# Turning the local q and k of two batches by DMA instead of on TensorE

## The chip, the cores and the metric

The kernel runs on one core of one Trainium2 chip. The metric is the device time of one execution in microseconds (us); lower is better. The time before is 301.74 us, the median of three runs that lie between 301.6 and 302.94 us. The profile is of one more execution.

## The reference

The work is a causal sparse attention followed by a two-layer network. There are 8 batches, 8 heads, 576 positions and 64 numbers per head. Heads 0 to 3 are local (a position sees the 32 positions that end with itself), heads 4 to 7 are strided (it sees the positions before it at multiples of 32).

```python
scores = scale * np.matmul(q, k.transpose(0, 1, 3, 2))
mask_local = (rel >= 0) & (rel < stride)                      # stride = 32, heads 0 to 3
mask_strided = (rel >= 0) & (pos[None, :] % stride == pos[:, None] % stride)   # heads 4 to 7
scores = np.where(masks[None, :, :, :], scores, -1000000000.0)
attn = np.exp(scores - max); attn = attn / (sum + 1e-09)
attn_out = np.matmul(attn, v)
x = attn_out.transpose(0, 2, 1, 3).reshape(4608, 512)
h = x @ w_in                                                  # 512 -> 2048
g = np.maximum(h, 0.0) + alpha * np.minimum(h, 0.0)
out = g @ w_out                                               # 2048 -> 512
```

## The kernel before

Batches, chunks and pairs are counted from 0 here, as the code does. (The change's own short name counts the batch whose load moves as the fourth; it is batch 3 here.)

**The two halves.** The 4608 tokens are cut into nine chunks of 512. Chunk n goes through the first layer in 16 `lin1_piece` calls (four matmuls of 512 columns each, L583; ScalarE makes `neg` at L591, VectorE makes `gT` at L594) and then through the second layer. Chunk 1 does that in 16 calls of `lin2_piece` (L622, four matmuls each); chunks 2 to 8 use `lin2_fast` (L708), which streams fewer columns but also needs the sums `gsum` that VectorE and GpSimd make (L652).

The attention of batch n+1 is done in small pieces between these calls: `attn_step` takes the next piece from a list, and the loop at the end of the kernel spreads the pieces evenly over a chunk. So the order on every engine is written out by hand, instruction by instruction, and each engine runs its own list in that order. An instruction that waits holds up all that stands behind it on its engine.

**Pairs.** Heads are worked on in pairs. Pair g belongs to batch g // 4; of a batch's four pairs, the first two (`hp` 0, 1) are local, the last two (`hp` 2, 3) strided. A pair's pieces are: scores (`score_both`, L353: matmuls of kT and qT, then ScalarE's exponentials at L376 and L382, then GpSimd's mask multiplies at L378 and L385), two or three "PV" pieces (`pv_piece`, L406, with VectorE's L413 and L415 behind), and the turn of the result into `xT`, by DMA transposes (`x_dma`: L446 straight into `xT` for local pairs, L443 into `xs` for pair `hp` 2, which ScalarE then orders into `xT` at L452) or, for `hp` 3, by TensorE and ScalarE (`x_piece`, L429 and L207).

**Where q and k come from.** Scores need q and k with the 64 head numbers on the partitions, so both must be turned. A local pair reads `qTs[0]` and `kTs[0]`; the first local pair of a batch uses half e = 0 of each, the second e = 1. Strided pairs read `qTs[1]` and `kTs[1]`. There are three ways in the kernel:

- Local q and k of batches 0 to 4: a load in fp32 by the SyncE (SP) or GpSimd queue (`load_qk`), a cast to 16 bits (`cast_l`, on GpSimd for batches 3 and 4), nine TensorE transposes for q and nine for k (`transpose_piece`, L269) into two PSUM tiles of the pool `ps` each, and two ScalarE copies each (L207) into `qTs[0]` or `kTs[0]`, which also put the columns in order.
- Local q and k of batches 5 to 7: a casting load on the GpSimd queue (`load_rows`, L116) and four DMA transposes on the SP queue (`turn_rows`, L128) that write `qTs[0]` and `kTs[0]` directly.
- Strided q and k of batches 3 to 7: a casting load of both on the GpSimd queue into `qsd` and `ksd` (`load_d`, L134, one buffer each), and two DMA transposes on the SP queue (`transpose_d`, L175).

**The places in the list.** For each g the list holds the scores of pair g, then the PV pieces of pair g-1, and for g+1 divisible by four the two transpose pieces `T(u, "q")` and `T(u, "k")` of the next batch between them. `run` adds side work to a piece: at g = 9 the casts of batch 3, at the last piece of g = 10 the load `load_d(3)`, at the last piece of g = 11 `transpose_d` for batch 3; the transposes of a local pair's result stand at the last piece of the next g. The list up to g = 11 and the turn of pair 11 is done within chunk 1, the list of batch 3 within chunk 2. `defer` holds ScalarE's second half of the exponentials back: one entry is taken at each following step.

Of the kernel before, what the change touches and what calls it, by code (L numbers as in the profile page):

```python
# [10 lines left out]
F16 = mybir.dt.float16  # L11
# [21 lines left out]
def kernel(  # L33
# [88 lines left out]
    def turn_rows(b):  # L122

        for nm in "qk":
            t16 = loaded[(b, False, nm)]
            for e in range(2):
                o = qTs[0][:, e, 0:576] if nm == "q" else kTs[0][:, e, 32:608]
                keep(nc.sync.dma_start_transpose(  # L128
                    o.rearrange("r (w p) -> r w p", p=96), t16[0:96, 768 * e : 768 * e + 768]))

    def load_d(b):

        for nm, src in (("q", q), ("k", k)):
            keep(nc.gpsimd.dma_start(  # L134
                qks[nm][0:72], src[b, 4:8, :, :].rearrange("h (p t) d -> p h (t d)", t=8)))
# [325 lines left out]
        pieces.append((g, fn))  # L461

    def T(u, nm):
        return lambda: transpose_piece(u, nm)

    def Sc(g, i):
# [8 lines left out]
    for g in range(7, npair + 2):  # L475
        c = g // 4
        a, p, t = g, g - 1, g + 1
        okA = 8 <= a < npair
        okP = 8 <= p < npair
        okT = 8 <= t < npair and t < 4 * NX and (t % 4 == 0 or t < 4 * DX and t % 2 == 0)  # L480
        nP = len(pairs[p].pgroups) if okP else 0
        seq = []
        if okA:
            seq.append(("S", lambda a=a: score_both(pairs[a])))
        if okP:
            seq.append(("P", Pv(p, 0)))
        if okT:
            seq.append(("T", T(t // 2, "q")))
        if 8 <= g - 2 < npair and not pairs[g - 2].xd:
            seq.append(("X", X(g - 2)))  # L490
        if okP:
            seq.append(("P", Pv(p, 1)))
        if okT:
            seq.append(("Tk", T(t // 2, "k")))
        if nP == 3:
            seq.append(("P", Pv(p, 2)))
        if not seq:
            seq.append(("N", lambda: None))

        todo = [(c, pr) for pr in range(2)] if g % 4 == 0 and 8 < g < npair else []  # L500

        if g % 4 == 1 and 9 <= g and c + 1 < B:
            todo = [(c + 1, nm) for nm in "qk"]
        lastP = max([i for i, z in enumerate(seq) if z[0] == "P"], default=len(seq) - 1)
        nslots = [i for i, z in enumerate(seq) if z[0][0] != "S"] or list(range(len(seq)))
        for i, (kind, fn) in enumerate(seq):
            extra = []
            if todo and i in nslots:
                left = len([z for z in nslots if z >= i])
                cnt = -(-len(todo) // max(1, left))  # L510
                extra = [todo.pop(0) for _ in range(min(cnt, len(todo)))]

            def run(fn=fn, extra=extra, g=g, c=c, kind=kind, lastp=(i == lastP), first=(i == 0),
                    second=(i == min(1, len(seq) - 1))):
                fn()
                for b, pr in extra:
                    if pr in ("q", "k"):
                        if b < NX:
                            cast_l(b, pr)
                        if b + 1 < NX:  # L520
                            load_qk(b + 1, pr)
                        continue
                    cast_v(b, pr, "pool")
                    if pr == 1 and b + 1 < B:
                        load_v(b + 1, True)
                if first and g % 4 == 2 and NX <= c + 1 < B:
                    turn_rows(c + 1)
                if lastp and g % 4 == 3 and NX <= c + 2 < B:
                    load_rows(c + 2, "k")
                if lastp:  # L530
                    if 4 * DX <= g - 1 < npair and pairs[g - 1].xd:
                        x_dma(pairs[g - 1])
                    if g % 4 == 3 and DX < c + 1 < B:
                        transpose_d()
                    if g % 4 == 2 and DX <= c and c + 1 < B:
                        load_d(c + 1)
                    if g % 4 == 1 and DX <= c and c + 1 < B:
                        load_v(c + 1, False)
                    if g % 4 == 1 and NX <= c + 2 < B:
                        load_rows(c + 2, "q")  # L540
                    if g == 8:
                        load_v(3, True)
                if second and 4 * DX <= g - 3 < npair and pairs[g - 3].xd and pairs[g - 3].strided:
                    after.append(lambda: x_copy(pairs[g - 3]))
            feed(run, g - 2 if kind == "X" else -1)
# [4 lines left out]

        return max(i for i, (g, _) in enumerate(pieces) if g == 4 * b + 3) + 1

    late, after = [], []

    def attn_step(end):
        while late:
            late.pop(0)()
        if pos["i"] < end:
            pieces[pos["i"]][1]()
            pos["i"] += 1  # L560
        if defer:
            defer.pop(0)()
        while after:
            after.pop(0)()

# [395 lines left out]
```

## Time and profile before

| | |
|---|---|
| time, median of three runs | 301.74 us |
| the profiled execution's own time | 301.52 us |
| its span in the profile | 299.7 us |
| busy in the span: TensorE (PE) | 293.2 us, 98% |
| VectorE (DVE), ScalarE (ACT), GpSimd (POOL) | 219.1, 178.6, 171.9 us |
| chunk 1, from its first to its last matmul | 57.50 to 92.15 us |
| chunk 2 | 92.15 to 123.62 us |
| chunk 3 | 123.62 to 153.94 us |
| granted TensorE clock | 0.998 |

The page gives busy times by engine, the chain of work that ended last, and groups of instructions by code line with the mean time of one. The timeline gives each engine's instructions in order, with the idle time before them and what ended it. "PEld" is TensorE's weight load, which lies beside its matmuls. DMAs are shown by when they were issued and how long they took from issue to landing; the DMA share is the mean busy share of the core's 16 DMA engines, and it goes over 1 where transfers overlap on an engine. Line numbers are those of the kernel before, unless the text says otherwise.

### The profile page before, as it was taken

How to read it: one execution, taken by the hardware profiler on the slowest of the kernel's cores; microseconds unless marked ns; L12 is line 12 of the kernel's file. 1: busy time of each engine (PE TensorE's matmuls, PEld its weight loads, DVE VectorE, ACT ScalarE, POOL GpSimd, SP SyncE). 2: the span in 40 equal slices, each digit the busy share in tenths (PEclk: the TensorE clock that was granted, in tenths of full speed). 3: DMA queues.
4: the chain of work that ended last, by engine and by line, in shares of the span. 5: the costliest groups of instructions: out<-in, count | busy, mean ns of one | idle time of the engine just before them, and what ended most of it. 6: DMA issues, size and time to landing. Idle time of an engine off the chain costs nothing.

```text
span 299.7 us, 6824 instructions
## 1 busy us (share of the span) xinstructions
PE 293.2 (98%) x2683; PEld 181.8 (61%) x2683; DVE 219.1 (73%) x408; ACT 178.6 (60%) x330; POOL 171.9 (57%) x160
## 2 busy tenths in 40 slices
PE   8999999999999999999999999999999999999995
PEld 3754545554544478646864686468745964684584
DVE  5677886668775897588848984898489948926852
ACT  1676755698457765776477647764676356416730
POOL 8362270049969998979897987595563305002300
PEclk9999999999999999999999999999999999999999
DMA  7999999999996969999989999966811140022004
GB/s 184 257 191 199 241 211 264 198 209 298 115 204 133 113 101 102 177 178 125 132 147 181 139 150 163 208 95 95 193 22 21 24 140 0 2 72 70 0 2 141
DMA packets 96976, 41.18 MB, mean 137 GB/s; under 512 B 75360, under 2 KB 93232, under 8 KB 96944
## 3 DMA queue, kind: packets, MB, share of 16 engines
q0 software_dynamic: 51008, 17.77, 59.0%
q1 hardware_dynamic: 45584, 22.32, 35.1%
q10 hardware_dynamic: 352, 0.66, 0.9%
q8 instruction: 21, 0.34, 0.5%
q14 instruction: 11, 0.09, 0.1%
HBM read 38.24 MB, written 9.44 MB: 159 GB/s over the span
## 4 chain that ended last, share of the span: by engine, by line
PE 84%; DVE 7%; ACT 4%; issue 2%; DMA 2%; SPq 0%; DVEq 0%; ACTq 0%
PE hps L583 37%; PE ops L708 24%; PE ops L622 5%; PE pv L406 4%; PE ops L864 3%; DVE gsum L652 2%; DVE gT L594 2%; PE sp L353 2%; DMA consts<-consts 2%; ACT neg L591 1%; PE xp L429 1%; PE sph L353 1%; DVE x L415 1%; PE ops L879 1%; ACT et L382 1%
## 5 line engine op out<-in xcount | busy, mean ns | idle before, releaser
L583 PE MATMUL hps<-xT,win 128*128 128x512 f16 x576 | 131.9, 379 | 0.2 <-ACT xT L452 0.2
L594 DVE SCALAR_TENSOR_TENSOR gT<-neg,oma,hps 128x512 f16<-128x512 f32 x144 | 105.3, 744 | 36.5 <-ACT neg L591 28.4
L591 ACT ACTIVATE neg<-hps 128x512 f32<-128x512 f32 x144 | 85.8, 598 | 35.7 <-PE hps L583 33.7
L583 PEld LDWEIGHTS <-win 128*128 128x128 f16 x576 | 53.7, 98 | 59.2 <-issue 0.5
L652 POOL TENSOR_TENSOR gsum<-gT 128x1024 f16<-128x1024 f16 x14 | 29.7, 2123 | 42.2 <-DVE gT L594 37.2
L378 POOL TENSOR_TENSOR et<-et,consts 128x576 f16<-128x576 f16 (+1 forms) x24 | 34.7, 1446 | 30.7 <-ACT et L376 30.5
L708 PEld LDWEIGHTS <-gsum 128*128 128x128 f16 x448 | 40.9, 98 | 7.3 <-DVE gsum L652 1.9
L708 PE MATMUL ops<-wsum,gsum 128*128 128x256 f16 x328 | 41.6, 273 | 0.3
L708 PEld LDWEIGHTS <-gT 128*128 128x128 f16 x336 | 31.5, 98 | 5.4 <-issue 0.3
L415 DVE TENSOR_TENSOR x<-pv,rc 96x384 f16<-96x384 f32 (+2 forms) x62 | 33.0, 532 | 2.1
L385 POOL TENSOR_TENSOR et<-et,consts 128x576 f16<-128x576 f16 (+1 forms) x24 | 31.4, 1309 | 0.0
L406 PEld LDWEIGHTS <-et 72*128 72x128 f16 (+1 forms) x448 | 23.4, 98 | 11.4 <-issue 1.8
L708 PE MATMUL ops<-wout,gT 128*128 128x256 f16 x224 | 27.9, 273 | 0.1
L376 ACT ACTIVATE et<-sp 128x576 f16<-128x576 f32 (+1 forms) x24 | 15.5, 644 | 17.1 <-PE sp L353 17.1
L413 DVE RECIPROCAL rc<-pv 96x6 f32<-96x6 f32 (+2 forms) x80 | 14.7, 183 | 10.6 <-PE pv L406 10.4
L211 POOL COPY vs<-stv 72x1024 f16<-72x1024 f16 x12 | 13.3, 1115 | 15.2 <-DMA stv<-in_v_dram 15.2
L663 DVE TENSOR_TENSOR osb<-ops,par 128x512 f32<-128x512 f32 (+1 forms) x14 | 9.4, 673 | 16.1 <-PE ops L708 8.2
L382 ACT ACTIVATE et<-sph 128x288 f16<-128x288 f32 (+1 forms) x48 | 18.8, 409 | 0.0
L661 ACT COPY osb<-ops 128x512 f32<-128x512 f32 x14 | 8.2, 585 | 16.8 <-PE ops L708 16.7
L622 PE MATMUL ops<-wout,gT 128*128 128x512 f16 x64 | 16.4, 379 | 0.0
L406 PE MATMUL pv<-vs,et 72*128 72x65 f16 x256 | 15.4, 193 | 0.8 <-ACT qT L207 0.5
L725 ACT COPY par<-ops 128x512 f32<-128x512 f32 x13 | 7.6, 585 | 14.1 <-PE ops L708 14.1
(105 smaller groups left out, 331.8 us busy)
## 6 DMA issues: line engine op xcount, KB each, us to landing
out_dram<-osb SPq DMA_DIRECT2D x35, 256.0 KB, 4.0
vl<-in_v_dram POOLq DMA_DIRECT2D x6, 384.0 KB, 9.3
win<-in_moe_w_in_dram POOLq DMA_DIRECT2D x4, 512.0 KB, 17.6
wout<-in_moe_w_out_dram POOLq DMA_DIRECT2D x4, 512.0 KB, 15.6
qsd<-in_q_dram POOLq DMA_DIRECT2D x7, 288.0 KB, 6.2
ksd<-in_k_dram POOLq DMA_DIRECT2D x7, 288.0 KB, 7.6
stv<-in_v_dram POOLq DMA_DIRECT2D x7, 288.0 KB, 7.8
ql<-in_q_dram SPq DMA_DIRECT2D x3, 576.0 KB, 7.3
```

The costliest lines, as they stand in the source:

```text
L376: keep(nc.scalar.activation(ev.rearrange("r (y c) -> r y c", y=2), sp[0:r, :, 0:n], AF.Exp, scale=SCALE))
L378: keep(nc.gpsimd.tensor_tensor(mv, mv, m, op=ALU.mult))
L382: keep(nc.scalar.activation(ev[:, n * y : n * y + n], sps[y][0:r, 0:n], AF.Exp, scale=SCALE))
L385: keep(nc.gpsimd.tensor_tensor(mv, mv, m, op=ALU.mult))
L406: keep(nc.tensor.matmul(pv[:, 65 * x : 65 * x + 65], et[0:r, c : c + 128], v16[0:r, 2 * P.pr + hh, t, :] if P.strided else v16[:, 6 * (2 * ...
L415: keep(nc.vector.tensor_tensor(P.x16[0:w, c0 : c0 + 64 * nb].rearrange("r (c e) -> r c e", e=64), pvv[:, :, 0:64], rc[0:w, 0:nb].unsqueeze ...
L583: keep(nc.tensor.matmul(hps, win16[:, kk, 128 * m : 128 * m + 128], xT[:, kk, c0 : c0 + 512], start=(kk == 2), stop=(kk == 1)))
L591: keep(nc.scalar.activation(neg, hps, AF.Relu, scale=-1.0))
L594: keep(nc.vector.scalar_tensor_tensor(gTs[n][:, m, :], neg, oma[:, m : m + 1], hps, op0=ALU.mult, op1=ALU.add))
L622: keep(nc.tensor.matmul(ops, gTs[n][:, kf, 128 * mt : 128 * mt + 128], wout16[:, kf, :], start=(kf == 0), stop=(kf == 15)))
L652: keep((nc.vector if eng == "dve" else nc.gpsimd).tensor_tensor(gsum[i][:, hs], a, b, op=op))
L708: keep(nc.tensor.matmul(o, lhs(y), rhs(y), start=(first and y == 0), stop=(y == 7), skip_group_check=True))
```

## The change

For batches 3 and 4 (`DX < b < NX`), `T(u, nm)` no longer issues TensorE transposes. Instead:

- `turn_cols(b)`, at the first piece of g = 10 (batch 3) and g = 14 (batch 4), issues on the SP queue one DMA transpose of the cast q and one of the cast k, 128 x 1152 numbers each, into new tiles `qx` and `kx` (one buffer each).
- Where the transpose pieces stood, the list `lazy` gets two ScalarE copies for q and two for k (`order_cols`, one for each half e), 128 x 576 numbers each, that read `qx` or `kx` with a step of 128 and write `qTs[0]` or `kTs[0]` in order. `attn_step` takes one of them at a step where `defer` is empty.
- `load_d(3)` moves from the last piece of g = 10 to the second piece of g = 11, and `transpose_d` of batch 3 from the last piece of g = 11 to the last piece of g = 12.

```diff
+    def turn_cols(b):
+
+        for nm in "qk":
+            t16 = hpool.tile([128, 9, 128], F16, tag=f"{nm}x", bufs=1, name=f"{nm}x")
+            keep(nc.sync.dma_start_transpose(t16, cast16[(b, False, nm)].rearrange("p t f d -> p (t f d)")))
+            cast16[(b, False, nm)] = t16
+
+    def order_cols(u, nm, e):
+
+        dst = qTs[u % 2][:, e, 0:576] if nm == "q" else kTs[u % 2][:, e, 32:608]
+        cast_copy("act", dst.rearrange("r (p t) -> r p t", t=9),
+                  cast16[(u // 2, False, nm)].rearrange("r t (p e) -> r e p t", e=2)[:, e])
...
     def T(u, nm):
+        if u // 2 > DX:
+            return lambda: lazy.extend([lambda: order_cols(u, nm, 0), lambda: order_cols(u, nm, 1)])
         return lambda: transpose_piece(u, nm)
...
+                if first and g % 4 == 2 and DX < c + 1 < NX:
+                    turn_cols(c + 1)
+                if second and g == 4 * DX + 3:
+                    load_d(DX + 1)
...
-                    if g % 4 == 3 and DX < c + 1 < B:
+                    if g % 4 == 3 and DX + 1 < c + 1 < B or g == 4 * DX + 4:
                         transpose_d()
-                    if g % 4 == 2 and DX <= c and c + 1 < B:
+                    if g % 4 == 2 and DX < c and c + 1 < B:
                         load_d(c + 1)
...
-    late, after = [], []
+    late, after, lazy = [], [], []
...
         if defer:
             defer.pop(0)()
+        elif lazy:
+            lazy.pop(0)()
```

In the order that results, ScalarE's list around the place in chunk 1 reads: last exponential of pair 11, q half 0, q half 1, k half 0, copy of an output tile (L627 before), k half 1, exponentials of pair 12. In chunk 2 it reads: the last two `neg`, q half 0, copy of `ops` (L722), q half 1, copy to `par` (L725), k half 0, k half 1, copy to `par`, exponentials of pair 16. On the SP queue `turn_cols(3)` stands between the transposes of pair 8's result and those of pair 9's, and `turn_cols(4)` between those of pairs 12 and 13. `load_d(3)` stands one mask multiply later on GpSimd, and `transpose_d` of batch 3 behind one more store of an output tile on SP. The scores of pair 12 wait for k half 0, those of pair 13 for k half 1.

## The prediction

> **What bounds the kernel now.** I read the page's busy shares and its chain first, then the timeline of each engine around the two places where the transposes stand, then the DMAs issued there.
>
> ```profile
> PE 293.2 (98%) x2683; PEld 181.8 (61%) x2683; DVE 219.1 (73%) x408; ACT 178.6 (60%) x330; POOL 171.9 (57%) x160
> ...
> PE 84%; DVE 7%; ACT 4%; issue 2%; DMA 2%; SPq 0%; DVEq 0%; ACTq 0%
> ```
>
> TensorE is busy 98% of the span and makes 84% of the chain: only what shortens TensorE's list, or makes it wait, moves the end. Its timeline around batch 3's transposes (start, us, form):
>
> ```profile
> 79.30 0.67 PE L269 MATMUL tp<-consts,ql 128*128 128x128 f16 x9
> 79.80 1.03 PE L622 MATMUL ops<-wout,gT 128*128 128x512 f16 x4
> ...
> 81.71 0.67 PE L269 MATMUL tp<-consts,kl 128*128 128x128 f16 x9
> 82.21 1.03 PE L622 MATMUL ops<-wout,gT 128*128 128x512 f16 x4
> ...
> 84.16 0.30 PE L353 MATMUL sp<-qT,kT 64*128 64x96 f16 x6
> ```
>
> There is no gap: each set of nine transposes takes 0.50 us of the list (79.30 to 79.80). ScalarE beside it (idle time in brackets):
>
> ```profile
> 79.77 1.36 ACT L207 COPY qT<-tp 128x640 f16<-128x640 f16 x2 [0.44 <-PE tp L269]
> 82.19 1.36 ACT L207 COPY kT<-tp 128x640 f16<-128x640 f16 x2 [1.05 <-PE tp L269]
> 83.41 0.60 ACT L627 COPY osb<-ops 128x512 f32<-128x512 f32 x1
> 84.57 0.65 ACT L376 ACTIVATE et<-sp 128x576 f16<-128x576 f32 x1 [0.56 <-PE sp L353]
> ```
>
> k is turned at 83.41, just before the scores of pair 12 at 84.16. ScalarE is idle for 2.05 us of this stretch, but its last copy is late.
>
> **Taken away.** Four sets of nine transposes, 4 x 0.50 = 2.0 us of TensorE, and eight copies of 0.73 to 0.76 us. Each set of nine counts in full only where TensorE waits for nothing else nearby.
>
> *Chunk 1 (batch 3):* second-layer matmuls without sums, no waits: 2 x 0.50 = -1.0 us.
>
> *Chunk 2 (batch 4):* VectorE limits the place.
>
> ```profile
> 109.94 2.16 PE L708 MATMUL ops<-wsum,gsum 128*128 128x256 f16 x16
> 111.93 0.67 PE L269 MATMUL tp<-consts,kl 128*128 128x128 f16 x9
> 112.44 1.07 PE L708 MATMUL ops<-wsum,gsum 128*128 128x256 f16 x8
> 113.59 0.30 PE L406 MATMUL pv<-vs,et 72*128 72x65 f16 x4
> ```
> ```profile
> 109.43 1.13 DVE L652 TENSOR_TENSOR gsum<-gT 128x1024 f16<-128x1024 f16 x1
> 110.48 2.36 DVE L652 TENSOR_TENSOR gsum<-gsum,gT 128x1024 f16<-128x1024 f16 x2
> ```
>
> The sixteen matmuls at 109.94 need the first sum (done about 110.5) from their fifth on; the eight at 112.44 need the third (done 112.84) from their fifth on. VectorE's list before them is unbroken from 106.52, so it does not get earlier. Without the q set, TensorE starts the sixteen at 109.44, does four in 0.44, waits until 110.5 and ends at 110.5 + 0.44 + 0.87 = 111.8, where it was 111.93. Without the k set, the eight start at 111.8, wait at their fifth until 112.84 and end at about 113.35, where PV began at 113.59. So 0.25 us of the 1.0 remains. Ends: 0, and 1.0 if the sums come earlier. I take -0.25, since chunk 3, with no transposes, has the same wait (its sixteen take 2.14).
>
> **Added: eight ScalarE copies from SBUF with a step of 128.** Nearest row of the groups by form, a copy that also gathers with a step, and the bounds:
>
> ```profile
> L452 ACT COPY xT<-xs 128x576 f16<-128x576 f16 x4 | 5.3, 1316 | 0.0
> L207 ACT COPY xT<-xp 128x576 f16<-128x576 f16 x8 | 5.1, 641 | 4.8 <-PE xp L429 4.8
> ```
>
> I take 1.32 us, 1.2 back to back (the two L452 copies at 90.11 take 1.41 together where their means add to 1.53, so 0.12 overlaps). Low end 0.64. No row has a step of 128 with runs of nine; I take 2.0 as the high end, half as much again. ScalarE's list grows by 8 x 1.32 - 5.96 = 4.6 us, with 40% idle to hide it, except where somebody waits: before the scores of pair 12.
> The Trainium skill (ScalarE: Activation LUTs, What ACT_TABLE_LOAD costs) gives an instruction with immediate operands as 186 ns + 0.833 ns per element, an estimate of 0.67 us here. The copy from PSUM agrees (641 ns), the gathering copy from SBUF does not (1316 ns), and the row decides; by the page's figure the copies would end as in the first rival below, with q at 81.5 at 301.0, and by the row at 302.9.
>
> **Added: four DMA transposes on SP.** SP issues one in 1.20 to 1.35 us. For batch 3 they stand behind pair 8's (second issued at 74.33 until 75.56) and behind the casts (GpSimd's k cast ends at 73.76): q issues at 75.65, k at 77.0. That is when the load of v has the DMA engines:
>
> ```profile
> 76.00:80.00 4.00, 4.00 (x51) 2.23 (x48) 3.45 (x6) 2.06 (x5) 3.98 (x5) 1.00 2.07 139
> 84.00:88.00 4.00, 4.00 (x44) 2.15 (x43) 2.84 (x7) 1.56 (x5) 2.71 (x3) 1.00 0.92 226
> ```
> ```profile
> vl<-in_v_dram POOLq DMA_DIRECT2D x1, 384.0 KB, 7.5
> xT<-x SPq DMA_TRANSPOSE x1, 6.1
> ```
>
> The first two rows are windows of busy time, their last column but one the DMA share; the other two are DMA issues with us to landing. The share is 2.07 here, 0.92 later. The load, issued at 73.72, lands 7.5 us on, at 81.2; a pair's transpose of a third of q's size, issued at 77.06, takes 6.1. Without such a load the qsd transpose, a little larger than q's (80 x 2048), takes 3.9 us (issued 85.80). So q lands between 75.65 + 3.9 = 79.6 and about 83 (the load's end, put off by q's own share). I take 81.5, 5.9 us after issue and near the loaded row, and k at 83.
>
> **What waits then.** ScalarE reaches q half 0 at 79.34 and is blocked until 81.5; behind it stand the output copy and pair 12's exponentials. q half 0, q half 1, k half 0 end at 81.5 + 1.2 + 1.2 + 1.32 = 85.2. TensorE, 1.0 us ahead, wants k at 83.16: a wait of 2.05 us (0.2 to 3.6 for landings of 79.6 to 83). Then ScalarE does the output copy (0.5), k half 1 (1.2) and pair 12's first exponentials (0.54 + 0.42), so the first `sph` tile is free 2.66 us after k half 0; the second PV piece of pair 11 needs that buffer 2.29 us after the scores (84.16 to 86.45): another 0.4 us.
>
> **Moved, and others behind them.**
> - Pair 9's transposes go behind q and k on SP, from 77.06 to 78.3 or later, landing about 87 instead of 85.4; chunk 2 reads them after 92.15. Hidden. `xs` of pair 10 (issued 84.46, 2.8 us) waits on SP for a store whose copy now follows k half 0: about 86.1, landed by 89; ScalarE wants it at 90.1 plus the shift. Hidden by about 2 us.
> - `load_d(3)` (0.79 and 0.70 us of GpSimd) steps behind one mask multiply, issued about 79.4 and 80.2 instead of 77.7 and 78.5; that mask is not needed before 85.4. It clears the DMA engines for q and k. `transpose_d` of batch 3 steps behind a store, from 85.80 and 87.24 to about 89.6 and 91; at 4 to 5.8 us it lands by 95 to 96.8, and the scores of pair 14 come at 96.59 plus about 1.5. Margin 1 us; if gone it costs at most the difference, a few tenths.
> - GpSimd's masks of pair 12 start 2.3 us later, and its list is unbroken from 85.29 to the sum that ends at 108.77. That sum then ends at 111.0; TensorE wants it at 110.9 and waits for VectorE until 112.0 anyway. Hidden.
> - Batch 4's q and k issue at about 99, under another v load, landing by about 107; ScalarE's slot is at 109. Hidden by 2 us. k half 0 ends near 113.7 plus the shift, pair 16's scores come at 114.4 plus the shift. Hidden by 0.7 us at 1.32 a copy.
>
> **Sum.** -1.0 + 2.05 + 0.4 - 0.25 = +1.2 us. On the profiled execution's own 301.52 (span 299.7 and 1.8 around it; 0.2 under the median of 301.74): 302.7, and 302.9 against the median, which I give. 0.5%, about 1.5 us, is what a measurement can tell from no change: 300.2 to 303.25.
>
> **The cases.**
> - *Forecast, 0.45:* k's half 0 is late by 1.1 to 2.9 us, 302.0 to 303.8. For it: the loaded DMA rows and L452.
> - *Rival, faster, 0.26:* the DMA transposes land before 80 and the copies run at 0.64. k half 0 then follows k's landing (81 to 82.3) at about 82.3 to 83, there is no wait, and -1.0 - 0.25 gives 300.5. If they land as I take, the cheap copies end at 83 + 0.64, a wait of 0.5: 301.0. With 1.32 copies it turns faster where q lands before about 80.3. Against it: 6.1 us for a third of the size. Span 300.2 to 302.0.
> - *Rival, all of it, 0.07:* as before, and VectorE's sums come earlier: 301.74 - 2.0 = 299.7. Against it: the same wait in chunk 3.
> - *Rival, much slower, 0.22:* a copy takes 2.0. k half 0 ends at 87.3, a wait of 4.1, the buffer 1.1 more, and in chunk 2 k half 0 ends at 115.3, past pair 16's scores by 0.9: -1.0 + 4.1 + 1.1 - 0.25 + 0.9 = +4.9, 306.6. Landings at 83 and 84.5 alone give 304.4. Span 303.8 to 306.6. Against it: it needs a copy dearer than any row, or both landings behind the v load's own.
>
> Faster is the third case and a little of the second (0.09); slower the fourth and a third of the first (0.36); the same 0.55. The range leaves out most of the third and the upper half of the fourth: 300.3 to 304.9. The forecast's own: 302.0 to 303.8.
>
> **What the profile after would show.** Right: no L269 after 65 us; ScalarE idle before the first qx copy with the DMA as its releaser; the copies near 1.3 us; TensorE idle about 2 us before pair 12's scores, released by ScalarE's kT copy; chunk 1 longer by 1 to 1.5 us, chunk 2 shorter by about 0.25. Wrong: TensorE unbroken at those scores (copies or landings cheaper than taken), chunk 2 shorter by 1 us, or a wait at pair 14's or 16's scores or at the start of chunk 2, where I have none.

## The result and the profile after

The changed kernel takes 309.64 us (median of six runs, 307.4 to 314.39) where the kernel before takes 301.68 us (301.6 to 302.94) beside it: a ratio of 1.0235 with a 95% interval of 1.021 to 1.0259. It is 2.35% slower; 302.9 us was forecast, and the range ended at 304.9. The run of 314.39 us, 2.3% above the fastest, is left out of the ratio, which is why it lies under that of the medians. The profiled execution took 308.36 us, its span is 306.4 us (before: 299.7). Line numbers are now those of the changed kernel: L366 are the scores, L419 PV, L643 `lin2_piece`, L604 `lin1_piece`, L220 a copy, L389 and L395 exponentials. In the experiments the lines of each run carry its own kernel's numbers.

The page of the kernel after, shares of busy time and the chain:

```profile
PE 294.0 (96%) x2647; PEld 180.8 (59%) x2647; DVE 218.0 (71%) x408; ACT 182.2 (59%) x330; POOL 173.0 (56%) x160
...
PE 75%; DMA 7%; ACT 6%; DVE 5%; issue 3%; POOL 2%; SPq 0%; DVEq 0%; ACTq 0%
```

TensorE has 36 instructions fewer but is busy 0.8 us longer, and its share of the chain fell from 84% to 75%. DMA and ScalarE are in the chain now. TensorE's timeline around pair 12's scores (start, us, form, idle time before and what ended it):

```profile
82.33 1.03 PE L643 MATMUL ops<-wout,gT 128*128 128x512 f16 x4
86.56 0.42 PE L366 MATMUL sp<-qT,kT 64*128 64x96 f16 x6 [3.20 <-ACT kT L220]
86.78 0.44 PE L366 MATMUL sph<-qT,kT 64*128 64x96 f16 x6
87.16 1.89 PE L643 MATMUL ops<-wout,gT 128*128 128x512 f16 x4
...
90.42 1.03 PE L643 MATMUL ops<-wout,gT 128*128 128x512 f16 x4
```

The wait for ScalarE's `kT` copy is there, 3.20 us long. Behind it the same four matmuls take 1.89 us that took 1.03 us before the wait, and 1.03 again from 90.42 on. ScalarE beside it:

```profile
79.07 0.41 ACT L395 ACTIVATE et<-sph 72x288 f16<-72x288 f32 x1
83.19 2.26 ACT L220 COPY qT<-qx 128x576 f16<-128x576 f16 x2 [3.71 <-DMA qx<-ql]
85.36 1.15 ACT L220 COPY kT<-kx 128x576 f16<-128x576 f16 x1
86.41 0.57 ACT L648 COPY osb<-ops 128x512 f32<-128x512 f32 x1
86.89 1.17 ACT L220 COPY kT<-kx 128x576 f16<-128x576 f16 x1
87.97 0.64 ACT L389 ACTIVATE et<-sp 128x576 f16<-128x576 f32 x1
```

It stands idle for 3.71 us until the DMA has brought `qx`, then does q half 0, q half 1 and k half 0 without a gap. The DMA issues between 74 and 96 us (kind, us from issue to landing):

```profile
vl<-in_v_dram POOLq DMA_DIRECT2D x1, 384.0 KB, 7.2
...
qx<-ql SPq DMA_TRANSPOSE x1, 7.4
kx<-kl SPq DMA_TRANSPOSE x1, 7.5
...
kT<-ksd SPq DMA_TRANSPOSE x1, 8.5
```

q was issued at 75.79 and landed at 83.16, k at 77.16 and 84.64. The clock, in the windows of busy time (after the five engines come the granted clock and the DMA share):

```profile
83.00:86.50 3.50, 0.36 (x2) 0.00 (x0) 1.86 (x2) 3.31 (x4) 0.78 (x1) 0.95 1.27 190
86.50:88.00 1.50, 1.44 (x15) 0.75 (x16) 0.00 (x0) 1.50 (x4) 0.00 (x0) 0.50 1.22 164
88.00:89.50 1.50, 1.50 (x10) 0.77 (x9) 0.09 (x1) 1.20 (x4) 0.82 (x1) 0.50 0.98 334
89.50:91.00 1.50, 1.50 (x13) 0.77 (x12) 1.00 (x4) 0.00 (x0) 1.50 (x3) 0.98 0.50 112
103.00:105.00 2.00, 2.00 (x6) 0.72 (x6) 0.00 (x0) 1.33 (x3) 1.98 (x3) 0.56 1.76 125
```

After the wait the clock is at 0.50 until about 89.5, and once more in chunk 2. The reason there is a second wait, at pair 14's scores:

```profile
98.55 1.89 PE L604 MATMUL hps<-xT,win 128*128 128x512 f16 x8
102.54 0.30 PE L366 MATMUL sp<-qT,kT 64*128 64x72 f16 x8 [2.10 <-DMA kT<-ksd]
102.68 0.30 PE L366 MATMUL sph<-qT,kT 64*128 64x72 f16 x8
102.91 4.45 PE L604 MATMUL hps<-xT,win 128*128 128x512 f16 x12
```

The moved strided transposes were issued at 92.53 and 93.99 and landed at 99.47 and 102.49. The twelve matmuls behind them take 4.45 us; the same twelve took 2.75 us at 95.78, at full clock.

**Where the time went.** A chunk is measured from its first L604 matmul to the next chunk's.

| | before | after | what lies in the difference |
|---|---|---|---|
| chunk 1 | 34.65 | 38.29 | -1.0 (transposes) + 3.2 (wait) + 1.45 (half clock, the rest) |
| chunk 2 | 31.47 | 34.09 | + 2.15 by pair 14's scores (the wait) + 1.7 by pair 15's (half clock) - 1.2 by pair 16's (transposes) |
| chunks 3 to 7 | 146.55 | 146.55 | nothing |
| ahead of chunk 1, and chunk 8 | 87.03 | 87.46 | + 0.43 (first loads 0.15, last stores 0.28) |

The sum is 306.4 us against 299.7.

### The profile page after: what moved, and what is told of

Same layout as the page of the kernel before. It is cut to its first block, busy times and chain, and to the rows that moved or that the text cites. A ratio compares the mean times of both kernels' runs of the same rounds, so it can differ in the third digit from the quotient of the medians.

```text
span 306.4 us, 6759 instructions
## 1 busy us (share of the span) xinstructions
PE 294.0 (96%) x2647; PEld 180.8 (59%) x2647; DVE 218.0 (71%) x408; ACT 182.2 (59%) x330; POOL 173.0 (56%) x160
## 4 chain that ended last, share of the span: by engine, by line
PE 75%; DMA 7%; ACT 6%; DVE 5%; issue 3%; POOL 2%; SPq 0%; DVEq 0%; ACTq 0%
PE hps L604 32%; PE ops L729 25%; PE pv L419 4%; PE ops L885 3%; DMA kT<-ksd 3%; DMA qx<-ql 2%; ACT neg L612 2%; DVE gT L615 2%; PE sp L366 2%; DMA consts<-consts 2%; PE ops L643 1%; ACT et L395 1%; PE xp L442 1%; DVE x L428 1%; PE sph L366 1%
## 5 line engine op out<-in xcount | busy, mean ns | idle before, releaser
L604 PE MATMUL hps<-xT,win 128*128 128x512 f16 x576 | 133.6, 383 | 0.2 <-ACT xT L465 0.2
L604 PEld LDWEIGHTS <-win 128*128 128x128 f16 x576 | 54.2, 98 | 60.5 <-issue 2.9
L391 POOL TENSOR_TENSOR et<-et,consts 128x576 f16<-128x576 f16 (+1 forms) x24 | 35.3, 1469 | 34.1 <-ACT et L389 33.1
L398 POOL TENSOR_TENSOR et<-et,consts 128x576 f16<-128x576 f16 (+1 forms) x24 | 31.9, 1328 | 0.3 <-POOL et L391 0.2
L419 PEld LDWEIGHTS <-et 72*128 72x128 f16 (+1 forms) x448 | 23.7, 98 | 11.7 <-issue 2.3
L389 ACT ACTIVATE et<-sp 128x576 f16<-128x576 f32 (+1 forms) x24 | 15.4, 644 | 18.4 <-PE sp L366 18.4
L395 ACT ACTIVATE et<-sph 128x288 f16<-128x288 f32 (+1 forms) x48 | 18.7, 407 | 0.0
L366 PEld LDWEIGHTS <-kT 64*128 64x128 f16 x392 | 8.7, 96 | 15.5 <-issue 8.2
L643 PE MATMUL ops<-wout,gT 128*128 128x512 f16 x64 | 17.1, 398 | 0.0
L419 PE MATMUL pv<-vs,et 72*128 72x65 f16 x256 | 15.6, 195 | 1.1 <-ACT qT L220 0.5
```

The costliest lines, as they stand in the source:

```text
L366: keep(nc.tensor.matmul(sps[y][:, w * x : w * x + w], P.kT[hf, k0 : k0 + 128], P.qT[hf, q0 : q0 + w], start=(x == 0), stop=(x == len(grp) ...
L391: keep(nc.gpsimd.tensor_tensor(mv, mv, m, op=ALU.mult))
L395: keep(nc.scalar.activation(ev[:, n * y : n * y + n], sps[y][0:r, 0:n], AF.Exp, scale=SCALE))
L398: keep(nc.gpsimd.tensor_tensor(mv, mv, m, op=ALU.mult))
L419: keep(nc.tensor.matmul(pv[:, 65 * x : 65 * x + 65], et[0:r, c : c + 128], v16[0:r, 2 * P.pr + hh, t, :] if P.strided else v16[:, 6 * (2 * ...
L604: keep(nc.tensor.matmul(hps, win16[:, kk, 128 * m : 128 * m + 128], xT[:, kk, c0 : c0 + 512], start=(kk == 2), stop=(kk == 1)))
```

## The experiments

Chunk times are those of the profiled execution, times are medians, and ratios, with their 95% interval in brackets, are against the kernel before on the same chip. Waits, landings and chunks are of one profiled execution per kernel, and landings differ between executions. The theory after the result: batch 3's q and k are late because the load of v has the DMA engines; TensorE's idle time then costs a second time by the half clock; the wait at pair 14 is a price of the moves. The rivals: the moves make q and k late; batch 4 has a part in it; the transposes are slow at this place whatever else is in flight; the slow matmuls come from something other than idle time.

**1. One batch at a time.** `cols_b4` does batch 4 alone and leaves the loads where they were; `cols_b3` does batch 3 alone, with the moves.

```diff
-        if u // 2 > DX:
+        if u // 2 == 4:        # cols_b3: == 3, and c + 1 == 3 below
...
-                if first and g % 4 == 2 and DX < c + 1 < NX:
+                if first and g % 4 == 2 and c + 1 == 4:
                     turn_cols(c + 1)
```

> Only batch 4's local q and k go by DMA transposes; batch 3 keeps its TensorE transposes, and the load and the transposes of batch 3's strided q and k stand where they stood before. Theory (the loss is two waits of TensorE in front of batch 3's scores, each followed by a stretch of half clock): no wait, clock 0.998, time between 300.7 and 301.5, that is 0.25 to 1.0 us under the kernel before. Rival (two more DMA transposes and two copies more in time cost wherever they stand): half of the 7.9 us lost, 305 or more.

Measured: 302.12 us, 1.001 [1.0001, 1.0019]. Chunk 2 takes 31.22 us where it took 31.47, but the time shows none of it.

> Only batch 3's local q and k go by DMA transposes, with the moved load and the moved transposes as in the changed kernel; batch 4 keeps its TensorE transposes. Theory: the whole loss is here, both waits and both half-clock stretches, 309 to 310.6. Rival (the cost is spread over both batches): about 305.5.

Measured: 308.83 us, 1.024 [1.0223, 1.0257]: all of the loss. TensorE waits 3.9 us at pair 12 and 1.2 us at pair 14; the half clock follows the first wait only, for 6.8 us. Batch 4 is harmless and gains nothing; the loss is batch 3's.

**2. The moves.** `moves_back` is the changed kernel with `load_d(3)` and batch 3's `transpose_d` in their old places. `moves_only` is the kernel before with only these two moves.

```diff
-                if second and g == 4 * DX + 3:
-                    load_d(DX + 1)
...
-                    if g % 4 == 3 and DX + 1 < c + 1 < B or g == 4 * DX + 4:
+                    if g % 4 == 3 and DX < c + 1 < B:
                         transpose_d()
-                    if g % 4 == 2 and DX < c and c + 1 < B:
+                    if g % 4 == 2 and DX <= c and c + 1 < B:
                         load_d(c + 1)
```

> Both batches by DMA transposes, but the load of batch 3's strided q and k and their two transposes back in their old places. Theory: the wait at pair 14's scores (2.1 us) and the half-clock stretch behind it (1.7 us) go, the wait at pair 12's scores stays at about 3.2 us or grows by up to 1 us because the load now shares the DMA engines with q and k: 305.5 to 307. Rival (the move is what lets q and k land at all in time): q lands 2 us or more later than 83.2, the wait at pair 12 is over 5 us, 308 or more.

Measured: 311.87 us, 1.0324 [1.029, 1.0358]: slower still. Its DMA issues between 72 and 96 us:

```profile
qsd<-in_q_dram POOLq DMA_DIRECT2D x1, 288.0 KB, 12.5
ksd<-in_k_dram POOLq DMA_DIRECT2D x1, 288.0 KB, 13.6
...
qx<-ql SPq DMA_TRANSPOSE x1, 8.2
kx<-kl SPq DMA_TRANSPOSE x1, 14.4
```

With three casting loads in flight k needs 14.4 us, and TensorE waits 9.4 us at pair 12. The theory's time fell short, since it did not reckon with this; the rival has the wait and the time, though not q: q lands at 84.17, only 1.0 us later than in the changed kernel, and k at 91.68, 7 us later. The move of the load is what let k land as early as it did, and does not cause the lateness.

> The kernel before with nothing but the moved load and the moved transposes of batch 3's strided q and k; all local q and k are turned by TensorE. If the wait at pair 14's scores is a price of the move by itself: the transposes issue at about 89.5 and 91, land at 96 to 98 beside the next v load's first half, and pair 14's scores (96.6 before) wait 0.5 to 1.5 us; 302 to 303.5. If it comes only with the DMA transposes of q and k and the clock stretch: no wait, 301.6 to 302.0.

Measured: 302.64 us, 1.0026 [1.0012, 1.004]. Its timeline at pair 14, where the kernel before has no gap:

```profile
98.35 0.30 PE L353 MATMUL sp<-qT,kT 64*128 64x72 f16 x8 [1.73 <-DMA kT<-ksd]
98.49 0.30 PE L353 MATMUL sph<-qT,kT 64*128 64x72 f16 x8
98.72 2.76 PE L585 MATMUL hps<-xT,win 128*128 128x512 f16 x12
```

The moves alone can bring the wait at pair 14. It is 1.73 us here, no half clock follows (2.76 us for the twelve matmuls), and the time is 0.9 us longer. The wait also needs a slow landing: `kT`, issued at 90.16, took 8.1 us here and 8.5 in the changed kernel. In the profiled executions of `filled` and `after_v_first` below, with the same moves, it took 4.6 and 4.2 us, and TensorE did not wait there.

**3. The half clock.** `filled` is the changed kernel with matmuls that write what is overwritten at once, put where TensorE waits: 12 ahead of pair 12's scores and 8 ahead of pair 14's.

```diff
+            if i == 0:
+                for _ in range({12: 12, 14: 8}.get(P.g, 0)):
+                    keep(nc.tensor.matmul(sp[:, 0], wrm[:, 0:128], wrm, start=True, stop=True))
```

> The changed kernel with idle work for TensorE: 12 matmuls of 512 columns of zeros in front of pair 12's scores (2.6 us) and 8 in front of pair 14's (1.7 us); they write the score tile, which the scores then overwrite. They add nothing where TensorE waits anyway. Theory (the half clock comes from the idle time): the clock stays at 1.0 behind both places, the waits themselves stay, 2 x 1.5 us less than the changed kernel, about 306.5. Rival (the half clock comes from something else that happens there, DMA traffic or a drop whatever TensorE does): still half clock for 3.4 us, 309.6.

Measured: 306.38 us, 1.015 [1.0131, 1.0169], a median 3.3 us below the changed kernel's. The windows of busy time where the changed kernel had 0.50:

```profile
86.50:88.00 1.50, 0.42 (x13) 0.35 (x14) 0.00 (x0) 1.50 (x3) 0.00 (x0) 1.00 1.21 159
88.00:89.50 1.50, 1.50 (x15) 0.79 (x14) 0.27 (x2) 1.50 (x3) 0.00 (x0) 1.00 1.10 224
```

The lateness of q and k is still there (they land at 84.19 and 86.04, about 1 us later than in the changed kernel, and TensorE waits 1.7 us behind the added matmuls), but the clock stays at 1.00. In all four executions the mean clock is 0.999 or 1.0, in the changed kernel's 0.994 or less. So the half clock comes from TensorE's idle time. What it is worth is less sharp: the table above has 1.45 and 1.7 us, together near the 3.3 us between the medians, while the two profiled executions differ by 1.7 us, with q and k later in this one and `kT` in time for pair 14.

**4. What makes q and k late.** Three kernels change only what is in flight beside the transposes. `v_later` is the changed kernel with batch 3's local v load just ahead of the moved `load_d(3)`; `after_v_first` has that load 11 us earlier instead, at the list's g = 7; `before_v_first` is the kernel before with the same early load (its condition reads `g == 7 and kind == "T"`; both issue the load at 63.0 us).

```diff
                 if second and g == 4 * DX + 3:
+                    load_v(DX + 1, False)        # v_later
                     load_d(DX + 1)
...
+                if first and g == 7:
+                    load_v(DX + 1, False)        # after_v_first
...
-                    if g % 4 == 1 and DX <= c and c + 1 < B:
+                    if g % 4 == 1 and DX < c and c + 1 < B:
                         load_v(c + 1, False)
```

> The changed kernel with batch 3's local v load issued five pieces later, just ahead of the moved load, so that nothing else loads while q and k are turned. If the v load is what made q and k late: q lands about 80 and k about 81.5 (4 to 4.7 us after issue, as such transposes take without a load), the wait at pair 12's scores is under 1 us, and no half-clock stretch follows it; v, q and k of the strided heads land later, about 87 to 90, and the wait at pair 14's scores may grow by a microsecond: 304 to 307. If the transposes are slow by themselves: q still lands at 82.5 or later and the wait stays over 2 us.

Measured: 306.1 us (303.27 to 306.17), 1.0121 [1.0077, 1.0165]. In the profiled execution, the fastest, q lands in 4.9 us and k in 4.4, TensorE waits 0.8 us at pair 12 and no half clock follows. The other three runs, at 306.1 us, have a mean clock of 0.994, what one spell of half clock would give; where it falls in them is not known. But `xs` of pair 10 now takes 7.3 us to land, beside the later load, and TensorE waits 1.0 and 0.5 us for it at the start of chunk 2. The lateness has moved.

> The changed kernel with only batch 3's local v load 11 us earlier. Theory: the v load is what made q and k late; they now land by about 80 and 81, no wait over 0.3 us at pair 12 and no half clock there; the wait of the moved strided transposes at pair 14 stays (0.9 us net, 1.7 alone): 301.8 - 1.0 - 0.25 + 0.9 = 301.4, 301.0 to 302.2. Rival: transposes at this place are late by themselves: q lands after 81.5, a wait of 2 us with the half clock behind it, 305 or more.

Measured: 303.96 us (302.5 to 307.0), 1.0081 [1.0051, 1.0112]. The waits of TensorE in its profiled execution (for what, us in total, times, longest):

```profile
PE sp L366 <- ACT kT L220: 1.3, 1, 1.3
PE ops L731 <- DVE gsum L675: 1.3, 2, 1.1
PE hps L606 <- ACT xT L465: 0.2, 1, 0.2
```

q and k land in 5.4 and 5.5 us, at 80.84 and 82.27, and the wait at pair 12 falls from 3.2 to 1.3 us. The time lies between the theory's and the rival's. With one edit 5.7 us of the 8 are gone, so the v load beside them is the main cause; the 5.7 hold the half clock, and the wait at pair 14, which did not come here. They are not as early as the theory had it (80 and 81): pair 8's transposes landed only at 78.6, with the early v load itself at 77.58.

> The kernel before with only batch 3's local v load 11 us earlier. Theory: TensorE waits for no transfer there, so nothing changes: 301.5 to 302.0. Rival: the earlier load takes the DMA engines from something that is needed: 302.3 or more.

Measured: 301.78 us, 1.0004 [0.9994, 1.0013]: the early load by itself does nothing.

**5. Turning them earlier.** `early_back` issues the two DMA transposes right behind GpSimd's k cast (q at 72.83 us instead of 75.79), with the moves undone; `early_b3` does that for batch 3 alone.

```diff
                         if b + 1 < NX:
                             load_qk(b + 1, pr)
+                        if DX < b < NX and pr == "k":     # early_b3: b == 3
+                            turn_cols(b)
```

> Both batches by DMA transposes, issued right behind the casts (the k cast of batch 3 ends at 73.8 us), ahead of pair 8's transposes and ahead of most of the v load, with the load and transposes of batch 3's strided q and k in their old places. Theory (the loss is the late landing): q and k land by about 78 and 80, ScalarE's copies end before 83.2, no wait at pair 12's or 14's scores, clock 0.998, time 300.5 to 301.0 (batch 3's 1.0 us gained, batch 4's about nothing, as when it was done alone). Rival (DMA engines are full around here, whatever the order): q and k still land after 81, a wait of 1 us or more stays, 303 or more.

Measured: 303.91 us, 1.0086 [1.0061, 1.0111].

> The same for batch 3 alone; batch 4 keeps its TensorE transposes. Theory: 300.6 to 301.0, within 0.3 us of the kernel with both. Rival (late whatever the order): 302.5 or more.

Measured: 303.51 us, 1.0063 [1.004, 1.0085]. In both q lands in under 4 us, ahead of the v load, k in 7.0 and 7.1, and TensorE does not wait at pair 12. In exchange the v load takes over 10 us, `xs` of pair 10 lands 3.6 us later than before (90.89 for 87.26, in `early_b3`), and TensorE waits 0.6 and 0.5 us (`early_b3`) at the start of chunk 2. That does not explain all: chunk 6, far from the change, takes 30.46 us instead of 29.38. `room` and, in part 6, `one_more` take the two things apart. `room` is `early_b3` without batch 3's local v load.

```diff
-                    if g % 4 == 1 and DX <= c and c + 1 < B:
+                    if g % 4 == 1 and DX == c:
+                        cast16[(c + 1, False, "v")] = vls[(c + 1) % 2]
+                    if g % 4 == 1 and DX < c and c + 1 < B:
                         load_v(c + 1, False)
```

> This is the kernel with the early transposes of batch 3 alone, and with batch 3's local v load left out (384 KB; its local heads then use batch 1's v, which is still in the buffer). Theory: what is left to wait for there is room on the DMA engines. Without the v load, q, k and xs of pair 10 all land in 3 to 5 us, TensorE waits neither at pair 12 nor at the start of chunk 2, and chunk 1 is 1.0 us shorter than before: 300.5 to 301.0, a span near 299 if chunk 6 stays at 29.3 (1.1 more if it does not). Rival: something other than the v load holds them (the order on SP, or the copies): a wait of 0.5 us or more stays at pair 12 or at the start of chunk 2, and the time is 301.7 or more.

Measured: 302.71 us, 1.0028 [1.0017, 1.0039]. Its DMA issues:

```profile
qx<-ql SPq DMA_TRANSPOSE x1, 3.5
kx<-kl SPq DMA_TRANSPOSE x1, 3.9
xs<-x16s SPq DMA_TRANSPOSE x1, 3.7
```

Here both theory and rival fall short. The landings are as expected (3.5 and 3.9 us where the changed kernel has 7.4 and 7.5), there is no wait for a transfer, and chunk 1 takes 33.63 us, 1.02 less than before: with room on the DMA engines the 1.0 us is there. But chunk 2 gives 0.57 us back and chunk 6 1.08, both as waits for VectorE's sums. For chunk 2 ScalarE and GpSimd have the reason:

```profile
84.05 0.65 ACT L389 ACTIVATE et<-sp 128x576 f16<-128x576 f32 x1
84.78 1.27 POOL L391 TENSOR_TENSOR et<-et,consts 128x576 f16<-128x576 f16 x1 [4.11 <-ACT et L389]
```

Pair 12's first exponentials stand behind the four copies, which with the output copy keep ScalarE busy without a gap from 79.16 to 84.05. So GpSimd's list, which begins with that pair's first mask, comes forward by 0.51 us only (84.78 where it was 85.29), and TensorE by 1.08 at the start of chunk 2. The difference is the 0.57.

`v_first` tried to get that room in a kernel that keeps the load: `early_b3` with the v load at g = 7 (and the extra copy of part 6).

> As the one before, and the load of batch 3's local v 11 us earlier, behind GpSimd's two `vs` copies of chunk 1's first quarter (about 62.9 us instead of 73.9). Theory: with the load over before q and k are turned, these land in 4 us, xs of pair 10 before 90, TensorE waits nowhere in chunk 1 or at the start of chunk 2, chunk 1 takes 33.6 to 33.7 us, chunk 2 31.4 to 32.0 and chunk 6 29.4: 300.5 to 301.2. Rival: the load only moves the crowd (onto the fp32 loads of batch 3's q and k, or the strided transposes): a wait of 0.5 us or more somewhere in chunk 1 or 2, and 301.8 or more.

Measured: 307.64 us (305.12 to 309.78), 1.0178 [1.0143, 1.0212]. Its DMA issues:

```profile
qsd<-in_q_dram POOLq DMA_DIRECT2D x1, 288.0 KB, 10.0
...
qx<-ql SPq DMA_TRANSPOSE x1, 7.8
kx<-kl SPq DMA_TRANSPOSE x1, 12.7
```

The rival held. The v load, now beside the fp32 loads of q and k, needs 13.7 us and is in flight until 78.3, when q should land; GpSimd, without the load's issue in its list there, comes to `load_d(3)` at 76.8 instead of 77.9, into k's transfer. k lands at 87.06 and TensorE waits 4.8 us.

**6. What comes back later.** The two gsum waits of `room` had an unlikely first sign: one `neg` (ScalarE) starts 0.28 us late in each of the two chunks, counted from the chunk's start, though the `hps` and `gT` that it needs are not later. It is number 192 and number 448 of ScalarE's instructions in the trace, with those that only wait for a semaphore counted. `one_more` is `early_b3` with one more small copy ahead of them, so that these numbers fall on others.

```diff
+        if u == 6 and nm == "q" and e == 0:
+            cast_copy("act", one, ident[:, 0:8])
```

> The kernel with the early transposes of batch 3 alone, and one more ScalarE copy of 8 columns from a constant into a tile that nobody reads, ahead of the first q copy. Theory: chunk 6 took 30.46 instead of 29.38 us because a ScalarE instruction whose number in the list is a multiple of 64 (448 here) starts 0.28 us late, and in that kernel it is the last `neg` of chunk 6; one more instruction puts the number on another one, chunk 6 takes 29.4 again and the time falls from 303.5 by 1.1 to 302.4. Rival: the early transposes themselves, or what they do to the order in time, make chunk 6 longer: it stays at 30.46 and the time at 303.5.

Measured: 302.84 us, 1.0037 [1.0025, 1.005], 0.7 us less than `early_b3` where 1.1 was expected; chunk 6 is back at 29.38 us. ScalarE's and VectorE's timeline of `early_b3` there,

```profile
229.35 0.60 ACT L612 ACTIVATE neg<-hps 128x512 f32<-128x512 f32 x1 [0.27 <-PE hps L604]
230.56 0.60 ACT L612 ACTIVATE neg<-hps 128x512 f32<-128x512 f32 x1 [0.61 <-DVE gT L615]
```
```profile
231.97 0.69 DVE L673 TENSOR_TENSOR gsum<-gT 128x1024 f16<-128x1024 f16 x1
232.58 3.44 DVE L673 TENSOR_TENSOR gsum<-gsum,gT 128x1024 f16<-128x1024 f16 x2
```

and the same places of `one_more`:

```profile
229.66 0.60 ACT L615 ACTIVATE neg<-hps 128x512 f32<-128x512 f32 x1 [0.33 <-DVE gT L618]
```
```profile
231.68 2.37 DVE L676 TENSOR_TENSOR gsum<-gsum,gT 128x1024 f16<-128x1024 f16 x2
```

The idle time before `neg` is 0.61 us in the one and 0.33 in the other. VectorE's two sums are 0.28 us later by it and take 3.44 us instead of 2.37. The places of GpSimd's two mask multiplies tell why. In `one_more` the first sum starts at 231.68, just ahead of the first mask at 231.71, and takes 0.68 us; the second starts within the mask and ends 0.55 us after the mask's end, 1.76 us in all. In `early_b3` the first sum starts at 232.58, behind the start of the mask at 232.34: now both sums start within a mask and take 1.76 us each. So 0.28 us became 1.08, and one instruction more, not the transposes, decides it. The effect is shown; why those instructions start late is not. The number alone does not do it: in the kernel before, number 448 is the `neg` ahead of that one, and it starts 14.19 us after the chunk's start, as in the others.

`room_more` is `room` with the same extra copy.

> The early transposes of batch 3 without batch 3's local v load (its local heads use batch 1's v), and with the one extra ScalarE copy. Theory: the v load's crowd and the late ScalarE instructions (numbers 192 in chunk 2 and 448 in chunk 6 of that list) are all that stood between taking 18 transposes away and the 1.0 us: chunk 1 33.6, chunk 2 31.5, chunk 6 29.4 us, no wait over 0.2 us, span 299 (up to 0.5 more for the last stores), 300.8 to 301.3. Rival: chunk 2 stays near 32 because GpSimd's list, which the change does not shorten, holds the sums there: 301.4 to 301.8.

Measured: 301.88 us, 1.0003 [0.9993, 1.0013]: no difference from before. Chunk 6 is 29.38 us, but chunk 2 stays at 32.18, as the rival had it. VectorE and GpSimd there:

```profile
108.76 0.76 DVE L678 TENSOR_TENSOR gsum<-gT 128x1024 f16<-128x1024 f16 x1
109.44 3.44 DVE L678 TENSOR_TENSOR gsum<-gsum,gT 128x1024 f16<-128x1024 f16 x2
```
```profile
106.82 2.14 POOL L678 TENSOR_TENSOR gsum<-gT 128x1024 f16<-128x1024 f16 x1
108.91 1.73 POOL L394 TENSOR_TENSOR et<-et,consts 72x576 f16<-72x576 f16 x1
110.61 1.71 POOL L401 TENSOR_TENSOR et<-et,consts 72x576 f16<-72x576 f16 x1
```

The kernel before has 2.36 us for those two sums. GpSimd's list, unbroken here from 87.72 to 115.2 us, did not come forward with TensorE: chunk 2 starts 0.7 us earlier than before and GpSimd's sum in it 0.2 us later (106.82 for 106.64), so 0.9 us later after the chunk's start. So VectorE's two sums now start within a mask multiply each, where the kernel before has its second sum behind both masks at 0.68 us, and TensorE waits 0.82 us. A transfer is in the way again, even without the v load:

```profile
82.11 1.20 ACT L223 COPY kT<-kx 128x576 f16<-128x576 f16 x1 [0.53 <-DMA kx<-kl]
```

Here k took 8.1 us to land where `room` has 3.9, and chunk 1 is 0.6 us shorter instead of 1.02. Where no transfer was in the way, in `room`, 0.45 us of the 1.0 were left after chunk 2. In the time, taking 18 transposes off TensorE's list in chunk 1 gives nothing that these runs can tell from no change.

**7. An attempt at a faster kernel.** `best` is `early_b3` with the first three pieces of chunk 2 begun with the quarters that do not read pair 10's result (kk = 0, 1), to hide the wait for `xs`; `best2` also has `load_d(3)` later; `order_only` is the kernel before with the order alone.

```diff
+        if n == 2 and m == 0:
+            for mm in range(3):
+                begun[mm] = phpool.tile([128, 512], F32, tag="hps", name="hps")
+                for kk in (0, 1):
+                    keep(nc.tensor.matmul(
+                        begun[mm], win16[:, kk, 128 * mm : 128 * mm + 128], xT[:, kk, c0 : c0 + 512],
+                        start=(kk == 0), stop=False))
```

> Early transposes of batch 3 alone, and at the start of chunk 2 the first two quarters (kk = 0, 1) of the first three pieces of the first layer go ahead of the quarters that read pair 10's result: these get 1.3 us more. Theory: the waits there (0.59 and 0.46 us with the early transposes) go, the 1.0 us of batch 3's transposes is left as a gain: 300.8 to 301.3, not over 301.6 unless chunk 6 again takes 1.1 us more. Rival: the other order only moves the wait (VectorE and ScalarE get the first sums 0.9 us later and the second layer waits for them): 302.0 to 302.6.

> As the one before, and with load_d(3) one mask multiply later, so that q, k and xs have the DMA engines alone for longer. Theory: xs of pair 10 lands 1 to 3 us earlier and no wait is left at the start of chunk 2; kT of the strided pairs lands later by about 1 us, so up to 0.9 us may come back at pair 14: 300.7 to 301.6. Rival: the wait at pair 14 that the moves alone had (1.73 us) comes back in full: 302 or more.

> The kernel before with only the other order of the first matmuls of chunk 2. Theory: pair 10's result is not late there, so the order gives nothing and costs nothing: 301.5 to 302.0. Rival: the first sums of chunk 2 come 0.9 us later and cost that: 302.3 to 302.7.

Measured: 304.36 us, 1.0079 [1.0063, 1.0096]; 305.0 us, 1.01 [1.0074, 1.0125]; and 302.78 us, 1.0031 [1.0021, 1.0042]. All three times lie in or past the rival's range (the first two also have the 1.1 us of chunk 6), but in `best2` not for the rival's reason: TensorE does not wait at pair 14 but at pair 12, since k took 9.6 us to land.

```profile
85.21 0.30 PE L366 MATMUL sp<-qT,kT 64*128 64x96 f16 x6 [1.70 <-ACT kT L220]
```

The three begun pieces hold all three buffers of the pool, the fourth waits 1.0 us for VectorE's `gT` in all three kernels, and `order_only` shows that this is the order's own price. No version here beats the kernel before.

## Why the prediction was wrong, step by step

- **What bounds the kernel** was right: the end moved with what TensorE waited for.
- **Taken away, chunk 1, -1.0:** right for the place (33.63 us in `room`, -1.02), wrong for the end. The step said the transposes count in full where TensorE waits for nothing near. It did not follow the gain into chunk 2, where VectorE's sums meet GpSimd's masks; in `room_more` chunk 1 is 0.6 us shorter and chunk 2 0.7 us longer. GpSimd was called hidden with a look at its own end (108.77 to 111.0), not at what VectorE's sums cost beside it. And ScalarE's longer copies were priced where TensorE waits for them, not where GpSimd's list does (`room`).
- **Taken away, chunk 2, -0.25:** right for the place, wrong for the end: `cols_b4` has -0.25 there, with waits of 0.6 and 0.2 us at the sums, and no gain in the time. In the changed kernel, where TensorE came late, 1.2 us came off there (the table above), which the lateness had paid for.
- **The copies, 1.32 us (1.2 back to back):** the nearest row was the right kind; they measured 1.15 to 1.22. The first rival's 0.64 and the fourth's 2.0 were both far off. The Trainium skill's figure (ScalarE: Activation LUTs, What ACT_TABLE_LOAD costs), an estimate of 0.67 us, does not fit these copies either.
- **The landing, 81.5 and 83:** too early by 1.7 us. q took 7.4 us, not 5.9, and landed just past the upper end of "79.6 and about 83". The sum used a row of a third of the size beside the same load and added nothing for the size. The cause named, the v load, was the right one (`after_v_first`, `room`).
- **The wait at pair 12, 2.05 us (0.2 to 3.6):** 3.20 measured, inside its bounds, with its mechanism and releaser as told; the size was off because the landing was. The extra 0.4 for the `sph` buffer did not show as a wait; TensorE was at half clock then and came later itself.
- **The margin of 1 us at pair 14, "a few tenths" if gone:** wrong, and a step that failed. `transpose_d` was issued at 92.5 and 94.0, not 89.6 and 91, because SP's list shifted with TensorE; kT took 8.5 us, not 5.8. The wait was 2.1 us. In `moves_only`, without that shift, it is still 1.73: kT, issued at 90.16, took 8.1 us to land.
- **What was not in the sum at all:** the half clock, about 3.2 us (1.45 and 1.7 in the table) of the 6.7 that were missed. This is the step that failed most: the prediction priced a wait of TensorE at its length, and the two waits, of 3.2 and 2.1 us, each cost about 1.5 us more.

By its own terms: -1.0 + 3.2 + 1.45 in chunk 1, where -1.0 + 2.05 + 0.4 stood, and +2.6 in chunk 2, where -0.25 stood. The fourth case (306.6, 0.22) came nearest in size, still 3 us short, and by copies of 2.0 us that did not come. Its other condition did come: for landings at 83 and 84.5 alone (83.16 and 84.64 measured) it had 304.4. The half clock and the wait at pair 14 are what lies between that and the measured time.

The Trainium skill (TensorE: Matmul & The Clock Gate, Why this matters for your kernels) asks for no idle gap over about 3 us between matmuls, and its section What's actually happening gives a free-running window of 3413 ns and half rate behind an idle one. By that rule the half clock could have stood among the cases for the long end of the forecast's waits (3.6 us), not for 2.05. The rate, the window and its free run agree with the trace (0.50, 3.413 us, the grid below). The threshold does not: 2.10 us of idle time was enough here.

## What to carry to other kernels

Price a wait of TensorE that could pass 2 us at its length and one spell of half clock behind it, and price a DMA transpose by the transfers in flight beside it: 3.5 to 3.9 us with room, 7.4 beside the load of v (8.5 in another execution), up to 14.4 beside three casting loads. Before counting time taken from the busiest engine as a gain, follow it to the next place where another engine's unbroken list meets it: what is earlier on one list is not earlier on the other. And a wait that is removed by moving a load may be paid by whatever stood where the load goes (`v_later`, `v_first`); look there first.

## What the runs showed of the hardware

- **The clock is set on a fixed grid.** The two spells of half clock of the changed kernel begin at 86.156 and 103.222 us, 17.066 us apart, five times 3.413, and each lasts 3.413; those of `cols_b3` and `moves_back` last two and three times that. Laid on that grid, the interval ahead of each has 2.79 and 2.10 us without a matmul. In the other kernels, an interval at full clock with 2.96 (`cols_b3`) or 3.41 us idle (`moves_back`, `v_first`) is followed by half clock, too, and one with 1.77 (`best`), 1.71 (`filled`), 1.70 (`best2`) or 1.48 (`moves_only`) is not. The closest two lie at the end of their kernels: 2.02 us idle (the kernel before) is followed by half clock, 1.88 (`room`) is not. Once at half clock, `cols_b3` stayed there for a second interval after one with only 0.92 us idle. Where a wait lies on the grid counts too: `moves_only` waited 1.73 us in all, over two intervals. This is also a likely reason, not shown, why kernels with waits near 2 us spread from 302.5 to 307.0 us (`after_v_first`) with mean clocks from 0.988 to 1.0, where the kernel before stays within 0.6 us beside them.
- **Casting loads and DMA transposes are slower beside each other.** The v load of 384 KB took 7.2 to 8.2 us in the kernel before, the changed kernel, `cols_b3` and `moves_back`, and 10.1 and 10.2 beside the early transposes of `early_back` and `early_b3`; but also 10.2 in `filled`, whose transposes are late, so executions differ as well. k's transpose, 288 KB of 16-bit numbers, took from 3.9 to 14.4 us in kernels that differ in the time of issue and in what else was in flight.
- **ScalarE's 192nd and 448th instruction started about 0.28 us late** in `room` and `early_b3`, 256 apart in the list; in the kernel before its 448th did not. One small instruction more ahead of them was worth 1.1 us at the end of chunk 6.
- **VectorE's sums and GpSimd's mask multiplies take turns.** A sum takes 0.68 us alone. One that starts while a mask multiply runs ends 0.55 us after that mask's end, in every case looked at: mask to 111.68, sum to 112.23 (before); 233.50 and 234.05 (`one_more`); 233.79 and 234.34, 235.47 and 236.02 (`early_b3`). The Trainium skill (GPSIMD Engine Reference, 8. Key points) says that GpSimd shares its SBUF interfaces with VectorE and contends with VectorE's instructions that have two SBUF inputs; the runs agree and give the size.
